# Six fill slots in place of eight for two projections, and the turned maxima kept out of one place of the pattern

## The chip, the cores and the metric

The kernel runs on one core of one Trainium2 chip. The metric is the device time of one execution in microseconds (us), as the median over runs.

## The reference

Of `x` (2048 tokens by 512) the reference computes full multi-head attention with 32 heads of 16, a small routed feed-forward path that touches two tokens, and a gate that mixes the two:

```
qkv    = x @ wqkv                               # 512 -> 3*512
scores = einsum("bhqd,bhkd->bhqk", q, k) * 0.25
p      = softmax(scores)                        # 2048 x 2048 for each of 32 heads
a      = einsum("bhqk,bhkd->bhqd", p, v) @ wo
r      = x @ w_r;  idx = the 2 tokens with the largest r
y      = (silu(x[idx] @ w_gate) * (x[idx] @ w_up)) @ w_down * sigmoid(r[idx])
b      = x, with y added at the two tokens
g      = sigmoid(sum(x * gate_w))
out    = g * a + (1 - g) * b
```

The bulk is the softmax attention: 32 matrices of 2048 by 2048 scores, each exponentiated, and each with its row maximum subtracted first.

## The kernel before

**Units and steps.** Two heads form a pair, and a pair with half of the queries (1024) is a unit; the last two pairs are cut into quarters instead. There are 32 units (`UNITS`). A unit takes 16 steps, one for each 128 keys, so there are 512 steps (`STEPS`). In a step, `s_piece` (L665) makes four score tiles of 128 keys by 512 queries (two heads by two blocks of 512 queries): one matmul into PSUM (`st`, three buffers), then an exponential on ACT into `P`. Two steps later `av_mm` (L676) multiplies `P` with the values: eight matmul instructions, four at a time side by side in column groups of the array, accumulated in `av` over the unit's 16 steps. When a unit is complete, `av_out` copies `av` out and `o_rows` sends it on by DMA.

**The maxima.** The subtraction of the row maximum is folded into the score matmul: the query operand `Qx` has two extra rows (48 and 49 of each head's half) that hold the negated maximum as a high and a low part, against rows of ones in the key operand. So a unit's maxima must be known before its first score tile. `m_piece` (L582) computes them some 21 steps ahead: 64 matmuls of 128 queries by 512 keys for each unit. They come in triples, numbered by `g // 3`: two matmuls into `mxa` (two banks, one buffer), reduced by one DVE instruction, and one into `mxb`, reduced by a second DVE instruction (both L596). When the 64 are done, `m_unit` (L641) reduces them once more on DVE and splits the result on POOL (`hl`). At the next triple, right behind the reduction of its `mxa` and ahead of that of its `mxb`, `m_rows` (L655) turns `hl` with a DVE transpose (L658) and issues eight small DMAs on SP's queue (L663) that write the two rows of `Qx` (`Qx<-hr`). With units numbered from 0, those whose number is a multiple of three have this turn in the third triple of a pattern, the others in the second or the fourth.

**The order.** The schedule is written out by hand. The main loop repeats a pattern of 28 entries (L31); in each, `s` is a score tile, `m` a maxima matmul, `A` the value matmuls of one step, and `f` one slot of fill work:

```
sssmmA smssmmA msssmmf smssmmAm
```

That is 12 score tiles (3 steps), 12 maxima matmuls (4 triples, starting where the pattern starts), 3 value steps and 1 fill slot. There are 164 patterns, numbered here from 0, then a tail without maxima from step 492 on, where a fill slot comes every second step. The third triple's `mm` is the one right ahead of `f`; its single `m` comes behind `f` and one `s`.

**The fill work** is one generator, `slots` (L875), of which each `f` takes one portion: the projections of the second, third and fourth group of queries and keys (12 matmuls each into the single buffer `fl`, handed out in portions of `piece`, L147 to L158), the feed-forward path, then the output projection of three groups of heads (`wo_groups`, 32 and 16 slots) and the pieces for the last group (`wo_last`, L567). Loads, splits on POOL and evictions hang on it by `at_step` and `late`, at distances counted from the slot. Before the change the first pieces of `wo_last` (four of 64 rows) stand in patterns 161 to 163 and in step 492, the nine of 128 rows in steps 494 to 510, three of them with a step before which they may not start (`wait`, L923). The results that the fill work reads are made at fixed steps: `split_last` (L544) writes the operand of `wo_last` at steps counted from the end of the attention units, on POOL and once on DVE. In the tail, and from step 490 on, `finish` (L560) adds a piece on DVE instead of on ACT and POOL.

**Small DVE work** waits in `gaps`. One item of it runs at the reduction of an `mxa` where neither an `m_unit` nor an `m_rows` stands (L599 to L604).

Of the kernel before, what the change touches and what calls it, by code (L numbers as in the profile page):

```python
# [36 lines left out]
def gated_mix(ctx: ExitStack, tc: tile.TileContext, xT, x, wqkv, wo, w_rg, w_gate, w_up, w_down,  # L37
# [12 lines left out]
    def st_tile(shape=(128, 512)):  # L50
        return psum.tile(list(shape), F32, tag="st", name="st", bufs=3)

    def fl_tile(shape=(128, 512)):
        return psum.tile(list(shape), F32, tag="fl", name="fl", bufs=1)
# [13 lines left out]
    def split(hi, lo, src, scale=None, lo_engine=None):  # L68
        if scale is None:
            nc.scalar.activation(hi, src, AF.Copy)  # L70
            (lo_engine or nc.vector).tensor_sub(lo, src, hi.bitcast(F32))
        else:
            nc.scalar.activation(hi, src, AF.Copy, scale=scale)
            nc.vector.scalar_tensor_tensor(lo, src, scale, hi.bitcast(F32), op0=OP.mult, op1=OP.subtract)
# [72 lines left out]
    def proj(g, which, nb, piece):  # L147
        i = "qk".index(which)
        wh, wl = W[g]
        ps = fl_tile() if g else st_tile()  # L150
        n = 0
        for terms in (((wh, xh), (wl, xh)), ((wh, xl),)):
            for c in range(4):
                for a, b in terms:
                    nc.tensor.matmul(ps, a[:, i, c, :], b[nb][:, c, :], start=n == 0, stop=n == 11)  # L155
                    n += 1
                    if n % piece == 0 and n < 12:
                        yield  # L158
        if g:
            if (g, which, nb) == (2, "q", 3):  # L160
                late.append((split_w, (3, (1,))))
                at_step(now[0] + 2, split_w, 3, (0,))
            late.append((evict, (g, which, nb, ps)))
            yield
            return
        ev = ev0(which, nb)
        scale = 0.25 if which == "q" else 1.0
        split(ev[:, 0], ev[:, 1], ps, scale=scale)
        first_rows(which, nb, ev)
        scr.append((0, which, nb, ev))  # L170
        if (which, nb) in (("k", 1), ("q", 2), ("q", 3)):
            if nb == 2:
                load_rows(0)
                load_rows(1)
            for e in scr[:2] if nb == 1 else scr:
                store_ev(*e)
            del scr[:2 if nb == 1 else 9]
        yield
# [3 lines left out]
    def ev0(which, nb):  # L182

        if (which, nb) in (("k", 1), ("k", 3)):
            t = ring.tile([128, 2, 2, 512], F32R, tag="xs", name="evx", bufs=2)
            evs.extend([t[:, 0], t[:, 1]])
        if evs:
            return evs.pop(0)
        return ring.tile([128, 2, 512], F32R, tag="ev", name="ev", bufs=2)

    def store_ev(g, which, nb, ev):
        e = ev.bitcast(F32)
        for i, src in ((0, e), (2, e[:, 0, :])) if which == "k" else ((0, e[:, 0:1, :].to_broadcast([128, 2, 512])), (2, e[:, 1, :])):
            d = ap(qk_scr[which], (g * 384 + i) * S + nb * 512, [[3 * S, 128], [S, 2 - i // 2], [1, 512]])
            nc.sync.dma_start(d.bitcast(F32), src)
# [16 lines left out]
    def first_rows(which, nb, ev):  # L212

        if which == "q" and nb > 1:
            return
        t = (Kx if which == "k" else Qx)[0][:, nb * 512:nb * 512 + 512].bitcast(F32)
        for j in range(2):
            e = ev[16 * j:16 * j + 16].bitcast(F32)
            two = e if which == "k" else e[:, 0:1, :].to_broadcast([16, 2, 512])
            queue = nc.gpsimd if j and (which, nb) in (("k", 1), ("k", 3), ("q", 1)) else nc.sync  # L220
            queue.dma_start(t[64 * j:64 * j + 32], two)
            queue.dma_start(t[64 * j + 32:64 * j + 48], e[:, 0 if which == "k" else 1, :])
# [57 lines left out]
    def k_of(u, c):  # L280

        return Kx[(u // 2) % 2 if u < QU else 2 * c]
# [33 lines left out]
    def load_rows(nb):  # L316
        if nb == 0:
            rg["w"] = o_tile("wr", [128, D]), o_tile("wg", [128, D])
            for i in range(2):
                nc.sync.dma_start(rg["w"][i], ap(w_rg, i * D, [[0, 128], [1, D]]))  # L320
        t = ring.tile([128, 4, D], F32, tag="P" if nb < 2 else "xs", name="xn", bufs=3 if nb < 2 else 2)
        nc.sync.dma_start(t, ap(x, nb * 512 * D, [[D, 128], [128 * D, 4], [1, D]]))
        rg[nb] = t
# [258 lines left out]
    def m_piece(g):  # L582

        u, e = divmod(g, EL)
        t, c, j = e // 8, e // 2 % 4, e % 2
        r = g % 3
        if r == 0:
            MX[0] = mxa_tile()
        elif r == 2:
            MX[1] = mxb_tile()  # L590
        dst = MX[0][:, r] if r < 2 else MX[1]
        nc.tensor.matmul(dst, Qx[u % 3][64 * j:64 * j + 48, t * 128:t * 128 + 128],  # L592
                         k_of(u, t // 4)[64 * j:64 * j + 48, c * 512:c * 512 + 512], start=True, stop=True)
        if r:
            g0 = (g - 1 if r == 1 else g) % (3 * EL)
            nc.vector.tensor_reduce(Mr[:, g0:g0 + (2 if r == 1 else 1)], MX[r - 1], axis=AX.X, op=OP.max, negate=True)  # L596
            if r == 1:

                if due:  # L599
                    m_unit(due.pop())  # L600
                elif turn:
                    m_rows(*turn.pop())
                elif e > 1 and e < EL - 1 and gaps:
                    gaps.pop(0)()  # L604
            if e == EL - 1 and r == 2 and u < UNITS - 1:
                due.append(u)
            elif e == EL - 1 or (e == 0 and r == 1 and g):
                m_unit(u if e else u - 1)
                if u == UNITS - 1 and e:
                    m_rows(*turn.pop())  # L610
# [42 lines left out]
    due, turn, gaps = [], [], []  # L653

    def m_rows(u, hl):  # L655

        r = ring.tile([128, 32], F32R, tag="hr", name="hr", bufs=2)
        nc.vector.transpose(r.bitcast(F32), hl.rearrange("p j i t -> p (j i t)").bitcast(F32))  # L658
        for j in range(2):
            for b in range(4):  # L660
                q = Qx[u % 3][64 * j + 48:64 * j + 50, :].rearrange("i (t n) -> i t n", n=128)
                p0 = 32 * b + 16 * j
                nc.sync.dma_start(q[:, :, 32 * b:32 * b + 32].bitcast(F32), r[p0:p0 + 16, :].bitcast(F32))  # L663
# [172 lines left out]
    def at_step(s, f, *a):  # L836
        fill.setdefault(s, []).append((f, a))
# [37 lines left out]
    def slots():  # L875
        for w, nb in order:
            yield from proj(1, w, nb, 3)
        late.append((split_w, (2,)))
        at_step(now[0] + 4, load_w, 3)
        x_rows()  # L880
        yield
        for w, nb in order:
            yield from proj(2, w, nb, 3)
        for n, (w, nb) in enumerate(order):
            yield from proj(3, w, nb, 3)
            if w == "q":
                for i in range(4):
                    at_step(now[0] + i + 1, load_ff, ("gate", "up")[i // 2], (w_gate, w_up)[i // 2],
                            ("xh", "xl")[i // 2], nb, i % 2)
        yield from ff_in("gate")  # L890
        for j in range(4):
            at_step(now[0] + 2 * j, load_down, j)
        ff_t(0, "gate")
        yield
        yield from ff_in("up")
        ff_t(1, "up")
        late.append((ff_act, ()))
        at_step(now[0] + 3, gaps.append, ff_h)
        at_step(now[0] + 3, load_wo)
        for c in range(4):  # L900
            at_step(now[0] + 6 + c, split_wo, c)
        at_step(now[0] + 5, load_at, 0, (0, 1))
        at_step(now[0] + 13, split_at, 0, (0, 1))
        yield
        yield
        yield from ff_down()
        ff_sum()
        last_tiles()
        s = now[0]
        for nb in range(4):  # L910
            at_step(s + 3 + 3 * nb, load_acc, nb)
        for t in range(16):
            at_step(s + 6 + t, acc_scale, t)
        yield
        yield from wo_groups((0, 1), (2,))
        assert now[0] > 3 * 8 * KT + 16
        yield from wo_groups((2,))
        for t in range(12, 16):
            wo_last(t, 64)
            yield  # L920
        for t in range(9):
            if t % 4 == 0:
                yield from wait((478, 494, 505)[t // 4])  # L923
            wo_last(t, 128)
            yield
# [138 lines left out]
```

## Time and profile before

| | |
|---|---|
| time, median of 3 runs | 1417.21 us (1416.7 to 1417.22) |
| the profiled execution | 1417.53 us, of which its span (first to last instruction) 1415.8 us |
| granted TensorE clock, mean | 0.999 |
| busy: PE, DVE, ACT, POOL | 99%, 91%, 83%, 22% of the span |
| the chain that ended last, by share | PE 99% |

PE is the matmul engine, PEld its weight loads, DVE, ACT and POOL the vector, scalar and general engines, SP the queue that issues most of the DMAs. A line of the timeline gives the start in us, the duration, the engine, the line of the kernel, the operation, what it writes and reads, its shape and how many were merged; in brackets stands how long the engine sat idle before it and what ended that. The ends of matmuls are modelled, so starts are the safer numbers on PE.

### The profile page before, as it was taken

To read this page: it belongs to the slowest core of one execution; us is meant where nothing else is said; L and a number is where in the kernel's file an instruction comes from. 1 tells how busy PE (TensorE), PEld (TensorE's weight loads), DVE (VectorE), ACT (ScalarE), POOL (GpSimd) and SP (SyncE) were. 2 spreads that over 40 slices of the span, in tenths; PEclk is the share of its full clock that TensorE was granted. 3 is DMA by queue.
4 is the path that set the end of the run, shared out by engine and by line. 5 is a ranking of instruction groups with operands and counts; after the bars stand their busy time and mean duration, and the time that the engine had idled before them with its cause. 6 is when DMAs were issued, how large, how long until landed. Compare 5 with 4: busy or idle time off the path is not lost.

```text
span 1415.8 us, 24079 instructions
## 1 busy us (share of the span) xinstructions
PE 1408.3 (99%) x9109; PEld 629.4 (44%) x9109; DVE 1288.4 (91%) x1536; ACT 1170.5 (83%) x2275; POOL 315.4 (22%) x334
## 2 busy tenths in 40 slices
PE   9999999999999999999999999999999999999998
PEld 6654444444444444444444444434444444444433
DVE  6889999999999999999999999999999999999943
ACT  5568888888888888888888888888888888888986
POOL 3841101102000001200000100043722322234410
PEclk9999999999999999999999999999999999999999
DMA  8712111312123221312222342414312131012012
GB/s 259 278 30 57 44 42 38 84 39 72 42 76 99 70 61 39 83 39 73 64 90 61 100 103 69 108 55 120 83 46 54 33 71 30 23 31 58 10 35 94
DMA packets 54775, 101.24 MB, mean 72 GB/s; under 512 B 13168, under 2 KB 20592, under 8 KB 53028
## 3 DMA queue, kind: packets, MB, share of 16 engines
q1 hardware_dynamic: 53940, 98.75, 24.7%
q8 instruction: 72, 1.18, 0.4%
q0 software_dynamic: 288, 0.30, 0.1%
q10 hardware_dynamic: 432, 0.66, 0.1%
q14 instruction: 43, 0.35, 0.1%
HBM read 63.77 MB, written 36.96 MB: 71 GB/s over the span
## 4 chain that ended last, share of the span: by engine, by line
PE 99%; DVE 0%; DMA 0%; ACT 0%; issue 0%; POOL 0%; DVEq 0%
PE av L682 36%; PE st L672 24%; PE mxa L592 12%; PE mxb L592 10%; PE fl L155 6%; PE fl L511 4%; PE st L301 3%; PE st L155 2%; PE mxa L627 1%; PE fl L402 1%; DMA ws<-wqkv 0%; PE fl L440 0%; DVE acc L562 0%; DVE Mr L596 0%; PE mxa L511 0%; PE mxb L627 0%
## 5 line engine op out<-in xcount | busy, mean ns | idle before, releaser
L673 ACT ACTIVATE P<-st 128x512 f32<-128x512 f32 x2028 | 1065.5, 599 | 190.8 <-PE st L672 100.5
L596 DVE TENSOR_REDUCE Mr<-mxa 128x2 f32<-128x1024 f32 x655 | 796.2, 1216 | 2.7 <-PE mxa L592 2.5
L682 PE MATMUL av<-P,V 128*32 128x512 f32 x4096 | 545.7, 605 | 0.0
L672 PE MATMUL st<-Qx,Kx 50*128 50x512 f32 x2028 | 537.5, 444 | 0.8 <-ACT P L673 0.6
L596 DVE TENSOR_REDUCE Mr<-mxb 128x1 f32<-128x512 f32 x654 | 451.1, 690 | 60.6 <-PE st L672 18.1
L672 PEld LDWEIGHTS st<-Qx,Kx 50*128 50x128 f32 x2028 | 279.3, 184 | 239.7 <-ACT P L673 223.7
L592 PE MATMUL mxb<-Kx,Qx 48*128 48x512 f32 x654 | 325.3, 497 | 0.0
L592 PE MATMUL mxa<-Kx,Qx 48*128 48x512 f32 x1310 | 294.1, 417 | 0.0
L592 PEld LDWEIGHTS mxb<-Kx,Qx 48*128 48x128 f32 x654 | 119.6, 183 | 273.5 <-DVE Mr L596 273.5
L682 PEld LDWEIGHTS av<-P,V 128*32 128x32 f32 x4096 | 81.2, 108 | 139.6 <-issue 133.5
L592 PEld LDWEIGHTS mxa<-Kx,Qx 48*128 48x128 f32 x1310 | 123.2, 183 | 44.5 <-DVE Mr L596 2.5
L208 POOL TENSOR_SCALAR ev<-pe 128x512 fp32r<-128x512 f32 x24 | 35.8, 1490 | 411.4 <-ACT pe L206 411.4
L478 POOL TENSOR_TENSOR acc<-acc,w 128x512 f32<-128x512 f32 x35 | 44.8, 1281 | 204.5 <-ACT w L477 204.5
L77 POOL TENSOR_SCALAR hl<-m 128x16 fp32r<-128x16 f32 x31 | 7.8, 253 | 296.8 <-DVE m L643 296.8
L155 PE MATMUL fl<-xh,wh 128*128 128x512 f32 x96 | 42.9, 447 | 0.0
L155 PE MATMUL fl<-xh,wl 128*128 128x512 f32 x96 | 40.4, 421 | 0.0
L511 PE MATMUL fl<-woh,ahl 128*128 128x512 f32 x96 | 35.2, 448 | 0.0
L562 DVE SCALAR_TENSOR_TENSOR acc<-fl,gg,acc 128x512 f32<-128x512 f32 x11 | 8.2, 747 | 28.0 <-PE fl L511 28.0
L632 DVE TENSOR_REDUCE Mr<-mxa 128x2 f32<-128x1024 f32 x21 | 25.7, 1224 | 8.4 <-PE mxa L627 8.4
L155 PE MATMUL fl<-xl,wh 128*128 128x512 f32 x96 | 32.6, 421 | 0.0
L303 ACT ACTIVATE V<-st 128x512 f32<-128x512 f32 x16 | 9.6, 600 | 26.5 <-PE st L301 26.5
L209 POOL TENSOR_TENSOR ev<-pe,ev 128x512 fp32r<-128x512 f32 x24 | 30.9, 1286 | 2.0
(189 smaller groups left out, 773.4 us busy)
## 6 DMA issues: line engine op xcount, KB each, us to landing
Kx<-k_scr SPq DMA_DIRECT2D x30, 384.0 KB
Qx<-q_scr SPq DMA_DIRECT2D x52, 192.0 KB
q_scr<-ev SPq DMA_DIRECT2D x15, 512.0 KB
k_scr<-ev SPq DMA_DIRECT2D x13, 512.0 KB
xn<-x SPq DMA_DIRECT2D x4, 1024.0 KB
Qx<-hr SPq DMA_DIRECT2D x256, 2.0 KB
acc<-x_scr SPq DMA_DIRECT2D x4, 1024.0 KB
q_scr<-ev SPq DMA_DIRECT2D x15, 256.0 KB
```

The source lines that it names most:

```text
L155: nc.tensor.matmul(ps, a[:, i, c, :], b[nb][:, c, :], start=n == 0, stop=n == 11)
L208: nc.gpsimd.tensor_scalar(ev[:, 0], t, 1.0, None, op0=OP.mult)
L209: nc.gpsimd.tensor_sub(ev[:, 1], t, ev[:, 0].bitcast(F32))
L301: nc.tensor.matmul(ps, a[nb][:, c, sl], b[:, c, :], start=c == 0 and n == 0, stop=c == 3 and n == 2)
L478: nc.gpsimd.tensor_add(a, a, w)
L511: nc.tensor.matmul(ps, a[:, sl], b[:a.shape[0], c, :], start=first and n == 0, stop=last and n == 2)
L592: nc.tensor.matmul(dst, Qx[u % 3][64 * j:64 * j + 48, t * 128:t * 128 + 128], k_of(u, t // 4)[64 * j:64 * j + 48, c * 512:c * 512 + 512], ...
L596: nc.vector.tensor_reduce(Mr[:, g0:g0 + (2 if r == 1 else 1)], MX[r - 1], axis=AX.X, op=OP.max, negate=True)
L632: nc.vector.tensor_reduce(*r, axis=AX.X, op=OP.max, negate=True)
L672: nc.tensor.matmul(ps, k, q, start=True, stop=True)
L673: nc.scalar.activation(P[s][:, 2 * j + c, :], ps, AF.Exp)
L682: nc.tensor.matmul(AV[0][32 * ct:32 * ct + 32, :], V[:, kt, h * VW:h * VW + 32], P[s][:, ct, :], start=kt == 0, stop=kt == KT - 1)
```

## The change

It has two edits. In `slots`, the first two projections of the fourth group (keys and queries of the first 512 tokens) hand out four matmuls to a slot instead of three; each takes three slots instead of four, and everything after them in the generator comes two slots (six steps) sooner. In `m_piece`, the turn is skipped in the third triple of a pattern and is made in the next one; the branch is taken all the same, so no item of `gaps` runs there in its place.

```diff
@@ m_piece
                 if due:
                     m_unit(due.pop())
                 elif turn:
-                    m_rows(*turn.pop())
+                    if g // 3 % 4 != 2:
+                        m_rows(*turn.pop())
                 elif e > 1 and e < EL - 1 and gaps:
                     gaps.pop(0)()
@@ slots
         for n, (w, nb) in enumerate(order):
-            yield from proj(3, w, nb, 3)
+            yield from proj(3, w, nb, 4 if n < 2 else 3)
             if w == "q":
```

## The prediction

> **What bounds the kernel now.** I read the page first, then the order of time inside single patterns, then the tail.
>
> ```profile
> PE 1408.3 (99%) x9109; PEld 629.4 (44%) x9109; DVE 1288.4 (91%) x1536; ACT 1170.5 (83%) x2275; POOL 315.4 (22%) x334
> ...
> PE 99%; DVE 0%; DMA 0%; ACT 0%; issue 0%; POOL 0%; DVEq 0%
> ```
>
> By this PE is everything, and then moving matmuls about would change nothing. But a busy PE on the page is not PE at its peak, so I look at the place that the change touches. Here are the third triple and the fill slot of one pattern with three fill matmuls, and the same reduction one pattern later:
>
> ```profile
> 643.95 0.50 PE L155 MATMUL fl<-xh,wh 128*128 128x512 f32 x1
> 644.18 1.21 DVE L596 TENSOR_REDUCE Mr<-mxa 128x2 f32<-128x1024 f32 x1
> 644.28 0.40 PE L155 MATMUL fl<-xh,wl 128*128 128x512 f32 x1
> 644.52 0.40 PE L155 MATMUL fl<-xl,wh 128*128 128x512 f32 x1
> 644.84 0.50 PE L672 MATMUL st<-Qx,Kx 50*128 50x512 f32 x1
> 645.45 0.51 PE L592 MATMUL mxa<-Kx,Qx 48*128 48x512 f32 x2
> 645.89 1.07 PE L682 MATMUL av<-P,V 128*32 128x512 f32 x8
> ...
> 647.42 0.69 DVE L596 TENSOR_REDUCE Mr<-mxb 128x1 f32<-128x512 f32 x1 [0.18 <-PE st L672]
> ...
> 651.89 1.21 DVE L596 TENSOR_REDUCE Mr<-mxa 128x2 f32<-128x1024 f32 x1
> ```
>
> The pattern takes 651.89 - 644.18 = 7.71 us. Within it the two banks of `mxa` decide here: their reduction ends at 644.18 + 1.21 = 645.39, the next pair of `mxa` matmuls starts at 645.45, and the value matmuls behind them at 645.89, which is 1.71 after the reduction began. In the rest of the pattern, with its three value steps, PE runs without a gap, and DVE waits for PE (the 0.18 in the fourth triple). So a pattern is PE for three triples, and a round trip PE, DVE, PE around the fill slot. If that is right, the slot's content hardly matters. One pattern with an empty slot (its third reduction starts at 922.08) and two with a wide fill of eight matmuls show it:
>
> ```profile
> 922.08 1.22 DVE L596 TENSOR_REDUCE Mr<-mxa 128x2 f32<-128x1024 f32 x1
> ...
> 923.79 1.06 PE L682 MATMUL av<-P,V 128*32 128x512 f32 x8
> ...
> 929.78 1.22 DVE L596 TENSOR_REDUCE Mr<-mxa 128x2 f32<-128x1024 f32 x1
> ...
> 937.48 1.21 DVE L596 TENSOR_REDUCE Mr<-mxa 128x2 f32<-128x1024 f32 x1
> ...
> 938.29 0.50 PE L672 MATMUL st<-Qx,Kx 50*128 50x512 f32 x1
> ...
> 939.19 1.07 PE L682 MATMUL av<-P,V 128*32 128x512 f32 x8
> ```
>
> Empty: 7.70 to the next reduction, and the value matmuls come 923.79 - 922.08 = 1.71 behind. Wide: 7.70 again, and 939.19 - 937.48 = 1.71, although the first score matmul after the fill starts at 0.81 (938.29 - 937.48) instead of 0.66 (644.84 - 644.18). The slot has room, and the wide fill nearly uses it up: 939.19 - 938.29 = 0.90 is the shortest way from that score matmul to the value matmuls that I find.
>
> **The change, part by part.**
>
> *Four matmuls in a slot, six times.* Inside a slot the matmuls follow at 644.52 - 644.28 = 0.24. A fourth puts the score matmul at 0.66 + 0.24 = 0.90 after the reduction's start, and the value matmuls at 0.90 + 0.90 = 1.80 instead of 1.71: 0.09 late. PE then has no gap until the next fill slot, so nothing gives it back, and the pattern is 0.09 longer. Six slots: +0.54 us. From below the cost is nothing, if the 0.90 can still shrink; I see no gain, since nothing is taken away there. From above it is the whole 0.24 for each, +1.4 us. I take +0.54, because 0.90 comes from the row nearest to the case.
>
> *Two slots fewer in the loop.* The matmuls stay 24, and an empty or a full slot gives the same 7.70. In the loop this part is worth nothing; what covers it is the `mxa` round trip. Entering and leaving a slot costs more than a step within it (644.28 - 643.95 = 0.33 at the entry, 644.84 - 644.52 = 0.32 at the exit). [...]
>
> *The tail.* There the freed slots count. Before, all ten slots of steps 492 to 510 are filled; after, wo_last's first piece of 128 rows moves into pattern 163, the others into steps 492 to 506, and steps 508 and 510 have none.
>
> ```profile
> 1364.22 0.73 PE L672 MATMUL st<-Qx,Kx 50*128 50x512 f32 x3
> ...
> 1365.89 0.50 PE L672 MATMUL st<-Qx,Kx 50*128 50x512 f32 x2
> ...
> 1366.33 0.74 PE L511 MATMUL fl<-woh,Kx 128*128 128x512 f32 x2
> ...
> 1368.65 0.72 PE L672 MATMUL st<-Qx,Kx 50*128 50x512 f32 x3
> ...
> 1369.18 1.58 ACT L673 ACTIVATE P<-st 128x512 f32<-128x512 f32 x3 [0.34 <-PE st L672]
> ```
>
> A step without fill takes 1365.89 - 1364.22 = 1.67, one with it 1368.65 - 1365.89 = 2.76. PE would gain 1.09 for a slot. But ACT has eight exponentials in these two steps and waits for PE only 0.34, so ACT takes over as the bound after that. I take the 0.34, twice: -0.68 us; the far end is PE's 1.09 twice, -2.2 us, the near end nothing. The swap of 64-row for 128-row pieces in pattern 163 and step 492 gives back what a 64-row piece overlaps with its neighbours; I allow 0.1 us and not more than one spacing of 0.24 in each. Two pieces of 64 rows are now added by ACT and POOL instead of DVE; ACT's waits of 0.34 and POOL's 22% hide them in the loop.
>
> *The turn, one triple later, for ten units (3, 6, ... 30).* This is a pattern that has one, with the same unit's first score matmuls and two small DMAs that show a round trip:
>
> ```profile
> 451.19 1.22 DVE L596 TENSOR_REDUCE Mr<-mxa 128x2 f32<-128x1024 f32 x1
> ...
> 452.32 0.20 DVE L658 STREAM_TRANSPOSE hr<-hl 128x32 f32<-128x32 f32 x1
> ...
> 452.90 1.06 PE L682 MATMUL av<-P,V 128*32 128x512 f32 x8
> ...
> 453.01 1.22 DVE L596 TENSOR_REDUCE Mr<-mxa 128x2 f32<-128x1024 f32 x1
> ```
>
> ```profile
> 452.55 5.30 SPq L663 DMA_DIRECT2D Qx<-hr  x8
> ```
>
> ```profile
> 461.62 0.73 PE L672 MATMUL st<-Qx,Kx 50*128 50x512 f32 x3
> ```
>
> ```profile
> 1377.41 0.39 SPq L763 DMA_DIRECT2D l_scr<-Ls  x1
> ...
> 1379.45 0.62 SPq L765 DMA_DIRECT2D rb<-l_scr  x1
> ...
> 1382.97 0.69 DVE L769 TENSOR_TENSOR an<-an,rb 64x512 f32<-64x512 f32 x1 [1.64 <-DMA rb<-l_scr]
> ```
>
> With the turn in place, the value matmuls come at 452.90 - 451.19 = 1.71, as without it: it costs nothing where it stands, so taking it away gains nothing. In the fourth triple DVE idles 0.18 and the turn takes 0.20: nothing again (at most 0.02 for each). A waiting `gaps` item runs one triple later, and nobody waits for it. What moves with the turn are its eight DMAs: 453.01 - 451.19 = 1.82 us later, behind whatever a step's end puts on SP; in the ten patterns I find nothing put there at that point. They occupy SP for 5.30, so the last is issued at about 452.55 + 5.30 - 0.66 + 1.82 = 459.0 (0.66 being 5.30 / 8). A small write went through in 1379.45 - 1377.41 = 2.04 (the load behind it waits for it), which gives 461.05: 0.57 ahead of the first score matmul at 461.62. The cover is thin; without it the rival below follows.
>
> *Fill work 15.4 us (two patterns) sooner against what it reads.* Two places are close:
>
> ```profile
> 1320.12 1.28 POOL L78 TENSOR_TENSOR lahl<-an,lahl 64x512 fp32r<-64x512 f32 x1
> ...
> 1323.48 0.73 PE L511 MATMUL fl<-woh,ahl 128*128 128x512 f32 x2
> ```
>
> ```profile
> 1386.16 1.29 POOL L556 TENSOR_TENSOR lahl<-an,lahl 128x512 fp32r<-128x512 f32 x1 [29.42 <-DVE lahl L555]
> ...
> 1388.42 0.74 PE L511 MATMUL fl<-woh,Kx 128*128 128x512 f32 x2
> ```
>
> The first 64-row piece now stands where the fill of pattern 159 stood (1323.48), 2.1 us after its operand is written (1321.40). The last 128-row piece now stands in step 506 (1388.42), 0.97 after its operand (1387.45). A wait here would stop PE, with all scores queued behind it; neither should occur.
>
> *Sum:* +0.54 - 0.68 + 0.1 + 0 = 0.0 us, on the profiled execution's 1417.53 (its span and 1.7 around it), which stands 0.3 above the median. I forecast the median unchanged: **1417.2 us**. With all prices at their ends it goes from -2.2 (tail by PE, the rest free) to +2.1 (1.4, two swaps at 0.24, ten turns at 0.02): 1415.0 to 1419.3.
>
> **The rivals.**
>
> *The turned rows land late (slower).* Place: the first score matmuls of ten units, on PE. The other round trip above, 1382.97 - 1379.45 = 3.5 us, puts the last landing at 462.5, which is 0.9 late, and PE stops for it ten times: +9 us, 1426. It decides from the point where a landing takes more than 461.62 - 459.0 = 2.6. For it: the thin cover. Against it: that load moves 128 KB and these rows 2 KB, so the 2.04 is nearer. With part of the lateness, say 0.3 to 0.6, it gives 1420 to 1423.
>
> *A fill matmul waits for its operand (slower).* One of the two margins, or one that I have not found, is gone: a stall of some 2 us at one place, 1419. The margins above speak against it.
>
> *PE bounds the tail (faster).* Then the two slots give 2.2, and with the fourth matmuls free 1415.0. ACT's small wait speaks against it.
>
> *The edit of the turn does nothing.* It would, if no unit turned in the third triple; the row at 452.32, between the reductions of that triple, excludes it.
>
> **How the numbers follow.** Forecast 70%, PE-bound tail 8%, a fill matmul waiting 8%, late rows 14%. The measurement can tell about 0.2%, 2.8 us, from no change. Within it lie the forecast, most of the PE-bound tail and most of a single wait: same 0.75. Late rows at 0.3 or more, with what two waits would give, are slower: 0.18. What is left of the tail's case, if the ten turns gained as well, is faster: 0.07. The range reaches from a tail bound by PE in part to the weaker end of the late rows: 1415.4 to 1420.4; the forecast's own is 1415.9 to 1418.9.
>
> **What would show it.** In the patterns with four fill matmuls, `av` starts about 1.80 after the third reduction, in the others 1.71. Steps 508 and 510 of the tail show ACT without the 0.34 wait. The first score matmuls of units 3, 6, ... 30 do not wait. A score matmul that waits for `Qx<-hr`, or a gap on PE before the fill of pattern 159 or that of step 506, would make the prediction wrong.

## The result, and the profile after

The changed kernel takes 1419.01 us (median of 22 runs, 1418.15 to 1425.0) against 1417.16 for the kernel before (22 runs, 1416.7 to 1417.62): a ratio of 1.0017, 95% interval 1.0011 to 1.0023. It is slower by 1.85 us, a small but clear loss, and its runs lie farther apart. The profiled execution took 1419.12 us. Three parts of its page:

```profile
span 1417.2 us, 24085 instructions
...
PE 1409.0 (99%) x9109; PEld 628.8 (44%) x9109; DVE 1288.1 (91%) x1534; ACT 1171.6 (83%) x2277; POOL 318.1 (22%) x336
...
PE 96%; POOL 2%; DMA 1%; DVE 1%; ACT 0%; issue 0%; DVEq 0%; SPq 0%; POOLq 0%
PE av L683 35%; PE st L673 23%; PE mxa L592 11%; PE mxb L592 10%; PE fl L155 6%; PE st L301 3%; PE fl L511 3%; PE st L155 2%; POOL acc L472 1%; DMA acc<-x_scr 1%; PE mxa L628 1%; PE fl L402 1%; DMA xs<-xT 0%; PE fl L440 0%; DVE Mr L596 0%; DVE acc L562 0%
```

The busy times are nearly those of before. The chain is not: before, it was PE from end to end; now POOL and a DMA hold 3% of it, with `acc L472` (`acc_scale`, the gate's factor on the accumulators) and the load `acc<-x_scr` behind it. The chain has found a place where PE waits for POOL. Comparing the starts of the patterns' first reductions in both timelines, pattern by pattern, finds it too. All but nine of the patterns behind the first (65 to 71, 109 and 115) take what they took before, within 0.05 us.

**Pattern 115.** In order of time, POOL and DVE of the changed kernel (the 0.22 reduction and the two `hl` are `m_unit` of unit 22, the transpose is its turn):

```profile
966.96 1.56 POOL L472 TENSOR_SCALAR acc<-acc,omg 128x512 f32<-128x512 f32 x1 [15.00 <-PE st L673]
...
972.95 0.73 POOL L505 TENSOR_TENSOR ats<-ats 128x256 f32<-128x256 f32 x1
...
977.87 6.19 POOL L472 TENSOR_SCALAR acc<-acc,omg 128x512 f32<-128x512 f32 x4
...
980.68 1.22 DVE L596 TENSOR_REDUCE Mr<-mxa 128x2 f32<-128x1024 f32 x1
...
984.03 1.29 POOL L478 TENSOR_TENSOR acc<-acc,w 128x512 f32<-128x512 f32 x1
...
985.30 3.11 POOL L472 TENSOR_SCALAR acc<-acc,omg 128x512 f32<-128x512 f32 x2
985.78 0.22 DVE L644 TENSOR_REDUCE m<-Mr 128x16 f32<-128x64 f32 x1
...
988.37 0.25 POOL L77 TENSOR_SCALAR hl<-m 128x16 fp32r<-128x16 f32 x1
988.71 0.22 POOL L78 TENSOR_TENSOR hl<-m,hl 128x16 fp32r<-128x16 f32 x1
...
988.96 0.21 DVE L659 STREAM_TRANSPOSE hr<-hl 128x32 f32<-128x32 f32 x1 [1.23 <-POOL hl L78]
...
989.66 1.21 DVE L596 TENSOR_REDUCE Mr<-mxa 128x2 f32<-128x1024 f32 x1
...
990.93 0.50 PE L592 MATMUL mxa<-Kx,Qx 48*128 48x512 f32 x2 [0.41 <-DVE Mr L596]
```

And the same place before:

```profile
977.68 1.57 POOL L472 TENSOR_SCALAR acc<-acc,omg 128x512 f32<-128x512 f32 x1 [10.93 <-PE st L672]
...
979.99 1.21 DVE L596 TENSOR_REDUCE Mr<-mxa 128x2 f32<-128x1024 f32 x1
980.90 3.11 POOL L472 TENSOR_SCALAR acc<-acc,omg 128x512 f32<-128x512 f32 x2
...
985.09 0.22 DVE L643 TENSOR_REDUCE m<-Mr 128x16 f32<-128x64 f32 x1
...
985.40 0.25 POOL L77 TENSOR_SCALAR hl<-m 128x16 fp32r<-128x16 f32 x1 [1.40 <-DVE m L643]
...
986.96 0.20 DVE L658 STREAM_TRANSPOSE hr<-hl 128x32 f32<-128x32 f32 x1
...
987.70 1.22 DVE L596 TENSOR_REDUCE Mr<-mxa 128x2 f32<-128x1024 f32 x1
```

Before, `m` is ready at 985.31 and POOL, idle for 1.40, takes it up at once. After, `m` is ready at 986.00 and `hl` starts at 988.37, because POOL is in the middle of `acc_scale`. DVE stands 1.23 us at its turn, PE behind DVE, and the pattern (980.68 to 989.66) takes 8.98 instead of 7.71 (979.99 to 987.70). The reason is order, not amount: each `acc_scale` hangs on a step counted from the fill slots, the maxima do not. Six steps sooner, nine of them (1 + 2 + 4 + 2, the second two at 969.88) are ahead of unit 22's `hl` instead of three (1 + 2). Six operations of `split_at` (972.95 to 977.87), which before came behind that `hl`, now stand ahead of it too (experiment 1 below leaves them there). And the nine cannot run early, since POOL's first one waits for its load. The "15.00 <-PE" is misleading there: that matmul has nothing to do with `acc`. A second profile of the same kernel (experiment 7 below) puts the same wait down to the load:

```profile
966.94 1.57 POOL L472 TENSOR_SCALAR acc<-acc,omg 128x512 f32<-128x512 f32 x1 [14.79 <-DMA acc<-x_scr]
```

SP's queue after and before shows when it is issued:

```profile
956.41 0.39 SPq L467 DMA_DIRECT2D acc<-x_scr  x1
...
968.60 1.54 SPq L467 DMA_DIRECT2D acc<-x_scr  x3
```

```profile
968.74 2.89 SPq L467 DMA_DIRECT2D acc<-x_scr  x3
```

The first load was 12 us sooner, and its first reader started 10.7 us sooner; but from 966.96 on POOL works without a pause until `hl`.

**The slots of four.** The first and the second of the six patterns, PE and DVE after:

```profile
597.50 1.21 DVE L596 TENSOR_REDUCE Mr<-mxa 128x2 f32<-128x1024 f32 x1
...
598.41 0.49 PE L673 MATMUL st<-Qx,Kx 50*128 50x512 f32 x1
...
599.31 1.06 PE L683 MATMUL av<-P,V 128*32 128x512 f32 x8
...
605.15 0.50 PE L155 MATMUL fl<-xh,wh 128*128 128x512 f32 x1
...
605.31 1.21 DVE L596 TENSOR_REDUCE Mr<-mxa 128x2 f32<-128x1024 f32 x1
...
606.28 0.49 PE L673 MATMUL st<-Qx,Kx 50*128 50x512 f32 x1
...
607.17 1.06 PE L683 MATMUL av<-P,V 128*32 128x512 f32 x8
...
613.18 1.21 DVE L596 TENSOR_REDUCE Mr<-mxa 128x2 f32<-128x1024 f32 x1
```

In the first, the score matmul starts 0.91 behind the reduction and the value matmuls 1.81 behind, where 0.90 and 1.80 were predicted. In the second it is 0.97 and 1.86, and the pattern takes 7.87 (605.31 to 613.18). From pattern 65 to 71 the lengths are 0.09, 0.17, 0.16, 0.19, 0.18, 0.05 and 0.05 over those of before: 0.89 for six slots.

**The tail.** Two steps at its end, now without fill, then its last stores after and before:

```profile
1396.98 0.73 PE L673 MATMUL st<-Qx,Kx 50*128 50x512 f32 x3
...
1401.06 0.73 PE L673 MATMUL st<-Qx,Kx 50*128 50x512 f32 x3
...
1401.60 1.57 ACT L674 ACTIVATE P<-st 128x512 f32<-128x512 f32 x3
```

```profile
1356.59 1.21 DVE L596 TENSOR_REDUCE Mr<-mxa 128x2 f32<-128x1024 f32 x1
...
1413.58 0.33 SPq L832 DMA_DIRECT2D out<-acc  x1
```

```profile
1354.63 1.22 DVE L596 TENSOR_REDUCE Mr<-mxa 128x2 f32<-128x1024 f32 x1
...
1412.06 0.33 SPq L831 DMA_DIRECT2D out<-acc  x1
```

The two steps take 1401.06 - 1396.98 = 4.08 instead of 4.43, and the exponentials no longer wait for PE. From the last maxima to the last store it is 56.99 instead of 57.43: -0.44.

The bill of this pair of profiles: +1.27 (pattern 115) + 0.89 (patterns 65 to 71) + 0.09 (108 and 109, 7.74 each instead of 7.70 and 7.69; why stays open) - 0.44 (tail) - 0.35 (the first pattern began at 89.24 instead of 89.59, ahead of any edit) = 1.46, against 1.4 between the spans.

### The profile page after: what moved, and what is told of

Read it like the earlier page. It is cut to its first block, busy times and chain, and to the rows that moved or that the text cites. A ratio compares the mean times of both kernels' runs of the same rounds, so it can differ in the third digit from the quotient of the medians.

```text
span 1417.2 us, 24085 instructions
## 1 busy us (share of the span) xinstructions
PE 1409.0 (99%) x9109; PEld 628.8 (44%) x9109; DVE 1288.1 (91%) x1534; ACT 1171.6 (83%) x2277; POOL 318.1 (22%) x336
## 4 chain that ended last, share of the span: by engine, by line
PE 96%; POOL 2%; DMA 1%; DVE 1%; ACT 0%; issue 0%; DVEq 0%; SPq 0%; POOLq 0%
PE av L683 35%; PE st L673 23%; PE mxa L592 11%; PE mxb L592 10%; PE fl L155 6%; PE st L301 3%; PE fl L511 3%; PE st L155 2%; POOL acc L472 1%; DMA acc<-x_scr 1%; PE mxa L628 1%; PE fl L402 1%; DMA xs<-xT 0%; PE fl L440 0%; DVE Mr L596 0%; DVE acc L562 0%
## 5 line engine op out<-in xcount | busy, mean ns | idle before, releaser
L472 POOL TENSOR_SCALAR acc<-acc,omg 128x512 f32<-128x512 f32 x16 | 24.8, 1565 | 15.0 <-PE st L673 15.0
```

The lines of the kernel that those rows point to most:

```text
L472: nc.gpsimd.tensor_scalar(a, a, omg[:, t:t + 1], None, op0=OP.mult)
```

## Experiments

The theory, called P: the loss is half POOL's queue, half the slots of four, less the gain in the tail; the turn is worth nothing. Its rivals: everything comes from the slots of four (F), or from the turn (T). Each experiment is set against the kernel before in the same round of measurements; its median there was 1417.23 us for experiments 1 to 4 and 1416.68 for 5 to 8.

**1. POOL's order alone, in the changed kernel.**

```diff
         for t in range(16):
-            at_step(s + 6 + t, acc_scale, t)
+            at_step(s + (6 if t < 2 else 13) + t, acc_scale, t)
```

> The changed kernel with fourteen of the sixteen acc_scale placed seven steps later, so that only two of them stand ahead of unit 22's hl in POOL's order; all else stays. Theory P (POOL's queue: hl of unit 22 stands behind acc_scale work that came late with its load, DVE waits for it in pattern 115, PE with it): pattern 115 goes from 8.98 back to about 7.71, the time falls by the 1.27 of the profiled stall to about 1417.7, and the spread of the runs (1418.15 to 1425.0) shrinks to that of the kernel before, some 1 us. Rival F (the four-matmul slots and the DMA traffic cost all of it): pattern 115 or one near it still loses over 1 us, 1419.0 with the same spread.

Measured: 1417.83 us (1417.57 to 1418.39, 11 runs), ratio to before 1.0004 (0.9995 to 1.0013). POOL and DVE in its pattern 115:

```profile
985.99 0.25 POOL L77 TENSOR_SCALAR hl<-m 128x16 fp32r<-128x16 f32 x1 [4.54 <-DVE m L644]
...
987.54 0.20 DVE L659 STREAM_TRANSPOSE hr<-hl 128x32 f32<-128x32 f32 x1
```

POOL now idles ahead of `hl` and the transpose has no wait. The pattern takes 7.71 again, the loss against the kernel before falls from 1.85 to 0.60, and the spread is 0.8 us. The same POOL instructions run; only their place in the queue differs. That settles the cause of the stall. The wide spread of the changed kernel's runs went with it, in half as many runs.

**2. The turn alone.** Against the changed kernel:

```diff
-            yield from proj(3, w, nb, 4 if n < 2 else 3)
+            yield from proj(3, w, nb, 3)
```

> The edit of the turn alone; all projections hand out three matmuls, the fill work is not moved. Theory of the prediction: the turn costs nothing in either place, 1417.2 as the kernel before, within 0.2. Rival T (the turned rows land late): the first score matmuls of units 3, 6, ... 30 wait, +0.3 to 0.9 for each, 1420 or more. If the turn was a burden in the third triple: 10 times up to 0.05, 1416.7.

Measured: 1417.17 us against 1417.23 (11 and 27 runs), ratio 1.0 (0.9991 to 1.0009). T falls. The turn is free in the third triple and in the fourth; the ten patterns that hold it sum to 77.65 us here and to 77.64 before. The rows do not land late either. In the changed kernel they are issued from 454.07 on, where before it was 452.55, and unit 9's first score matmuls follow on the value matmuls of 460.29 without a gap:

```profile
454.07 5.30 SPq L664 DMA_DIRECT2D Qx<-hr  x8
```

```profile
460.29 1.07 PE L683 MATMUL av<-P,V 128*32 128x512 f32 x8
...
461.30 0.74 PE L673 MATMUL st<-Qx,Kx 50*128 50x512 f32 x3
```

**3. The slots of four alone, with the later work where it was.** Against the changed kernel:

```diff
             yield from proj(3, w, nb, 4 if n < 2 else 3)
+            if n == 1:
+                yield
+                yield
```

> The changed kernel with two empty slots behind the two projections, so that all later fill work stands where it stood before. It leaves the six slots of four matmuls and the edit of the turn. By the trace of the changed kernel, six slots of four with what spills into the next pattern cost 0.9: 1418.1, no stall in pattern 115, a spread as small as before. By the price of the prediction (0.09 each) 1417.7. If the stall belongs to the four-matmul slots or to the turn (rival F): 1419 or more with a spread of several us.

Measured: 1418.19 us (11 runs) against 1417.23: +0.96, ratio 1.0007 (0.9998 to 1.0016). No stall in pattern 115 (it takes 7.71). The interval alone does not exclude no change, but its profile has +0.93 in patterns 65 to 71, and no other pattern behind the first is longer than before by 0.05. By the medians the six slots cost 0.16 each, near what the trace had, and not the prediction's 0.09; experiment 5 shows this clear of the noise. Against experiment 1 it lacks the two freed slots of the tail and is 0.36 slower, as the two profiles have it (57.39 us from the last maxima to the last store, against 56.99); as a difference of times alone, that is within the noise.

**4. POOL's order alone, in the kernel before.**

```diff
         for t in range(16):
-            at_step(s + 6 + t, acc_scale, t)
+            at_step(s + 4 + 3 * (t // 4), acc_scale, t)
```

> The kernel before with nothing but acc_scale placed sooner: the four of one load at once, right behind that load, so that eight instead of three stand ahead of unit 22's hl in POOL's order. Theory P: POOL has 8 x 1.55 + 1.3 of work from about 977.7 on, hl comes near 991 instead of 985.4, DVE and PE lose some 4 us in pattern 115, about 1421, with runs apart by us. Rival (the order on POOL does not matter): 1417.2 as before.

Measured: 1424.49 us (1423.19 to 1425.71, 5 runs), ratio 1.0053 (1.0039 to 1.0067). The kernel before falls into the same hole when eight `acc_scale` stand ahead of `hl`:

```profile
991.03 0.21 DVE L658 STREAM_TRANSPOSE hr<-hl 128x32 f32<-128x32 f32 x1 [4.16 <-POOL hl L78]
```

The stall is the expected 4 us (pattern 115 takes 11.92), but the kernel loses 7.3 in the median, and 6.0 in the profiled execution, the fastest of the five. Pattern 116 takes 9.45, and nothing there waits for POOL. The table of stretches shows what differs there; its columns are the stretch, its length, the busy time of PE, PEld, DVE, ACT and POOL with their counts, then the granted clock, the DMA share and GB/s:

```profile
985.00:988.90 3.90, 3.84 (x27) 1.13 (x25) 1.86 (x3) 3.06 (x7) 3.90 (x3) 1.00 0.00 0
988.90:990.50 1.60, 0.00 (x0) 0.00 (x0) 0.00 (x0) 0.57 (x1) 1.60 (x3) 1.00 0.00 0
990.50:991.80 1.30, 0.00 (x0) 0.00 (x0) 0.77 (x3) 0.00 (x0) 1.12 (x4) 0.51 0.00 0
991.80:996.90 5.10, 5.03 (x19) 1.81 (x19) 3.45 (x5) 1.54 (x3) 4.85 (x6) 0.50 0.02 4
996.90:998.00 1.10, 1.10 (x5) 0.57 (x3) 0.93 (x2) 1.10 (x3) 1.10 (x2) 0.79 0.12 28
```

```profile
991.87 0.79 PE L592 MATMUL mxb<-Kx,Qx 48*128 48x512 f32 x1 [3.02 <-DVE Mr L596]
...
993.72 1.93 PE L682 MATMUL av<-P,V 128*32 128x512 f32 x8
```

After PE's gap of 3.02 the granted clock is half, and the eight value matmuls take 1.93 instead of 1.07. That the halved clock is the whole of pattern 116's loss fits, but no run separates it.

**5. The price of a slot of four, doubled twice.** All eight projections of the last group, each with an empty slot behind it, against the changed kernel:

```diff
-            yield from proj(3, w, nb, 4 if n < 2 else 3)
+            yield from proj(3, w, nb, 4)
+            yield
```

> All eight projections of the last group in three slots of four matmuls, each followed by one empty slot, so that everything stands where it stood before; the edit of the turn is in. 24 slots of four instead of 6. If each costs 0.09 (the prediction's price): +2.2, 1419.4. If each costs 0.15 with what spills into the next pattern, as the trace of the changed kernel shows for six in a row: +3.6, 1420.8. No stall in pattern 115 and a small spread in either case.

Measured: 1420.57 us (7 runs) against 1416.68: +3.89, ratio 1.0028 (1.0017 to 1.0039), for 24 slots 0.16 each. The price scales with the number of slots. It also depends on what stands ahead: here an empty slot ends each group of three, and in the profile the first pattern of a group is 0.07 to 0.12 longer than before, the second 0.06 to 0.18, the third 0.15 to 0.28, and the one with the empty slot 0.01 to 0.04.

**6. The price of fill work in the tail, in the kernel before.** The nine pieces of 128 rows keep one matmul of three; the products with the low parts are left out.

```diff
-        wo_terms(ps, ah[:k], al[:k], 3, slice(tt * 128, tt * 128 + 128), True, True)
+        if k == 128:
+            nc.tensor.matmul(ps, ah[:k, tt * 128:tt * 128 + 128], wop[0][:k, 3, :], start=True, stop=True)
+        else:
+            wo_terms(ps, ah[:k], al[:k], 3, slice(tt * 128, tt * 128 + 128), True, True)
```

> The kernel before, with one matmul instead of three in the nine pieces of 128 rows (the low parts of operand and weight are left out in them, so ten slots of the tail have almost the same shape and less PE work). Two steps then take PE 4.43 - 2 x 0.24 = 3.95. If ACT is the bound after its wait of 0.34 is gone (the prediction's price), the nine slots give 9 x 0.34 = 3.1: 1414.1. If PE bounds the tail all the way: 9 x 0.48 = 4.3: 1412.9. If the tail is hidden: 1417.2.

Measured: 1414.38 us (11 runs) against 1416.68: -2.30, ratio 0.9984 (0.9975 to 0.9993), 0.26 for each slot. That is nearer to ACT's 0.34 than to PE's 0.48, and below both. Some of ACT's wait stays, at every second fill slot, as in this row of its tail:

```profile
1368.13 1.57 ACT L676 ACTIVATE P<-st 128x512 f32<-128x512 f32 x3 [0.21 <-PE st L675]
```

So ACT takes over as the bound once PE has less to do, and one matmul left in a slot still gets in its way.

**7 and 8. The changed kernel twice more,** for the link between span and stall.

> The changed kernel itself, for another profiled execution. Theory P: the span follows the stall of pattern 115. Where hl of unit 22 comes later than in the first profile (988.37), the pattern is longer than 8.98 by as much and the span than 1417.2 too; where it comes sooner, shorter. Rival: the spread comes from elsewhere, the pattern stays at 8.98 while the span moves.

> The changed kernel itself, a third profiled execution; the same expectations: span and pattern 115 move together (theory P), or the span moves without it (rival).

Measured: spans of 1417.2 and 1416.9. Pattern 115, POOL's `hl` and DVE's turn in each:

```profile
988.36 0.25 POOL L77 TENSOR_SCALAR hl<-m 128x16 fp32r<-128x16 f32 x1
...
988.95 0.21 DVE L659 STREAM_TRANSPOSE hr<-hl 128x32 f32<-128x32 f32 x1 [1.01 <-POOL hl L78]
```

```profile
988.22 0.25 POOL L77 TENSOR_SCALAR hl<-m 128x16 fp32r<-128x16 f32 x1
...
988.82 0.21 DVE L659 STREAM_TRANSPOSE hr<-hl 128x32 f32<-128x32 f32 x1 [1.53 <-POOL hl L78]
```

The expectation missed. The stall varies (the pattern takes 8.77 and 9.29), but the longer stall goes with the shorter span. `hl` comes at 988.2 to 988.4 in all three executions: it stands at the end of a POOL queue that begins with the landing of a load. How early DVE arrives there varies, and the stall is the difference: an execution that was ahead loses its lead. What made 1421 to 1425 of a few runs was not profiled. Their granted clock is on record, though: 0.996 in the two longest runs (1424.14 and 1425.0), 0.999 or 1.000 in the other twenty, the one of 1421.31 among them; in the five runs of experiment 4 it is 0.996 or 0.997. So in the two longest the clock fell much as it did there. That a longer stall in pattern 115 was the reason would fit but is only argued.

No version that keeps all products is faster than the kernel before (experiment 6 leaves some out). Freeing a tail slot costs three slots of four (some 0.45) and gives some 0.2 (0.44 for two), so experiment 1, without the stall, is still 0.6 above the kernel before in the median, though its interval does not exclude no change.

## Why the prediction was wrong

The forecast of 1417.2 (no change) is refuted: the measured interval lies wholly above 1. The measured 1419.01 lies in the wide range given (1415.4 to 1420.4) and just outside the forecast's own (1415.9 to 1418.9). That it is in the wide one says little for the sum: its largest cost stands in none of the terms.

*The step that failed* is "Fill work 15.4 us (two patterns) sooner against what it reads". It asked of each moved piece of PE work whether its operand is there in time, found two narrow places, and both held (after the change the operands are written at 1320.89 and 1389.61, their matmuls start at 1325.33 and 1390.58). It did not ask what the POOL work that moves with the slots now stands ahead of. The sixteen `acc_scale` were not even costed: the term stood at nothing, and the profile has 1.27 us for it in pattern 115, which experiment 1 gives back. POOL's 22% stood as proof that it has room, while the question was the order in one queue over 20 us, with a load at its head. The rival of a single stall ("or one that I have not found", 2 us, 1419) had the number, but on a matmul's operand, and at 8%; that 1419.01 is so near it is luck as well, since the total also holds the fours and the tail.

*The four matmuls* were right in mechanism and mis-sized: +0.54 predicted, 0.89 in the trace and 0.96 in experiment 3. The 0.09 is what the first slot costs. The next four cost 0.16 to 0.19: each follows a pattern that ended late on PE, and its fill starts only 0.16 ahead of the reduction (605.15 against 605.31), where the prediction's row has 0.23. The groups of three in experiment 5, where the first slot is on average the cheapest and the third the dearest, bear this out. The price was taken for one slot and multiplied.

*The empty slots in the loop* gain nothing, as was said: in experiment 5 the patterns with an empty slot are no shorter than with a full one (0.01 to 0.04 longer).

*The tail* was right in sign and cause and nearly in size: -0.68 and 0.1 back predicted, -0.44 in the trace. Experiment 6 puts a slot at 0.26 with one matmul still in it. The two steps without fill take 4.08 instead of 4.43, so ACT takes over, as was said, and PE's gain of 1.09 for each slot is excluded. That a 64-row piece overlaps with its neighbours shows in the profile of before, where a score matmul starts at 1339.18, between the matmuls of such a piece (from 1338.80 on and at 1339.26); the 0.1 for it was an estimate, and no run has it by itself.

*The turn* was right: nothing, in both places (experiment 2), and the rival of the late rows is excluded by the same run. Of the signs that were to show the prediction wrong, none came; none of them looked at POOL.

## What to carry to other kernels

When a bundle of background work is moved, list for each engine (POOL too) what the bundle now stands ahead of in its order, and who waits for that. Here unit 22's `m` was ready at 986.00, and its `hl`, behind `acc_scale` work that had begun with a load (POOL idle for 14.79 before it in experiment 7), started at 988.37; with fourteen of the sixteen placed later it started at 985.99 (experiment 1). A share of busy time over the whole span says nothing of that: POOL's is 22% before and after. A cost that repeats is priced where the work repeats, not for the first instance: measure two in a row.

## What the hardware showed

In experiment 4 a stall of PE was followed by a halved clock. PE stood idle for 3.02 us, with nothing from 988.90 on; the granted clock was 1.00 from there to 990.50, 0.51 from 990.50 to 991.80, still ahead of PE's next matmul at 991.87, and 0.50 until 996.90, and pattern 116 took 1.7 us more. In the first profile of the changed kernel, whose stall leaves PE idle for about 0.5 us (busy 2.49 of the 3.00 from 988 to 991), the clock stays at 1.00.
